# Two batch-0 products and k^T v in quarters of TensorE, lam*beta1 added to the token mix's input, beta2 as a 321st column

## Chip, cores and metric

One core of one Trainium2 chip. The metric is the device time of one execution, in microseconds (us). Engines are named as the profile names them: PE is TensorE (PEld its weight loads), DVE is VectorE, ACT is ScalarE, POOL is GpSimd, SP is SyncE, whose queue issues nearly all DMAs.

## What is computed

Linear attention with a norm per head, followed by a residual MLP-mixer block, for 8 batches, 8 heads, 576 positions, head width 64, model width 512 and hidden width 2048, all in float32 at the borders:

```python
kv = einsum('bhsd,bhse->bhde', k, v)
out = einsum('bhsd,bhde->bhse', q, kv)
x = out / sqrt(mean(out*out, -1) + 1e-6) * g_norm        # to [8, 576, 512]
a1 = alpha1 * x + beta1
u = x + lam * einsum('ts,bsd->btd', w_tok, a1)           # token mix
a2 = alpha2 * u + beta2
y = u + lam * (maximum(a2 @ w_ch1, 0) @ w_ch2)           # channel mix
```

## The kernel before

The kernel is a list of operations that `Prog.op` records with an engine, an estimated cost and the keys read and written; `Prog.plan` simulates the list with those costs several times, gives every operation a priority from how late it may run, shakes the priorities at random by a list of seeds, and fixes the order of each engine's queue and its waits. So every engine runs a fixed order, and a change of any cost or seed may reorder all of it. Where PE has nothing ready before the first channel-mix matmul, the planner puts in matmuls on a tile of zeros (`warm`, L1429).

Each batch goes through these steps. `load_kv` and `load_q` fetch k, v and q: 512 positions in one DMA per tensor (L538, L505), the last 64 positions ("tails") in DMAs of their own (L543, L512; L530 for batch 0). `kv_groups` forms k^T v in fp32: two groups of 16 matmuls with 128 rows and 64 columns (L691; each fp32 matmul shows as two instructions), then one group for the tails in quarters of 64 rows and 64 columns (L701), and ACT and DVE copy the result as a bf16 pair, high and low part (L718, L723, L726). q is split into such a pair (`split_q`, L501 and L582) and transposed, by PE for batch 1 (L605), by SP's transposing DMA from batch 2 on (L591). `qkv_groups` multiplies both (L782 with a second matmul on held weights at L401, tails at L863) and normalizes: square on ACT (L819), sum on DVE (L821), root on ACT, reciprocal on DVE, the normalized x (L840, tails L884), then `rt` or `rtt` = x times alpha1*lam*g in bf16 on DVE (L844, tails L892), and x times g_norm in place on POOL (L848, L895). `rtt` holds the 64 tail rows of even batches in its lower half and those of odd batches in its upper half; one row of the other half holds lam*beta1, and the token weights' matching row holds the row sums of w_tok (`sums`, L1301), so that the fifth 128-row source chunk of the token mix brings in the constant too.

`tok_groups` is the token mix: for two pairs of output chunks five source chunks each, 10 matmuls of 512 columns per pair (L920), and in odd batches one group for the tail rows of both batches, in column halves (L942). DVE adds x (L927), multiplies by alpha2 (L933), and SP's DMA transposes the result to `a2t` (L1037); batches 0 and 1 are transposed on PE instead (`ut_pe`, L1007, evicted at L1016 and L1017). `ch1_groups` is the first layer: 16 groups of 4 matmuls of 512 columns in even batches (L1056), of 8 matmuls of 320 columns in odd ones (L1075), which also take the tails of the batch before; ACT applies the ReLU with the bias `hb` from batch 2 on (L1045, L1046). `hb`, beta2 times w_ch1, is formed in batch 0 with a one-column matmul after each of L1056 on the same weights (`matmul_held`, L401). `ch2_groups` is the second layer (L1121, 64 or 80 matmuls a batch) with the addition (L1131) and the store (L1134). The steps of batch b+1 up to its transposed input are merged among the layers of batch b.

Batch 0 has no layers to hide behind. Its k, v and q come in two halves of four heads. `kv_first` already runs in quarters of TensorE (L628). `qt_first` transposes q by matmuls with the identity, 128 rows by 64 columns (L649; tails L663), and the products q x kv (L789) use a block-diagonal `kv32` that is zeroed at the start. Then come the transposes of w_tok (L1260, L1278; loads L1219 and L1222), the token mix in two column halves (`tok_first`, L972), and the transposes of its result. The weights of both layers are loaded to borrowed buffers and cast (L1340, L501) or multiplied by lam (L1351, L1357).

## Time and profile before

| | us |
|---|---|
| median of 3 runs (368.4 to 368.56) | 368.47 |
| the profiled execution, its own time | 368.05 |
| its span, first to last instruction | 366.2 |
| PE busy, of that span | 360.6 |
| DVE / ACT / POOL busy | 198.4 / 159.2 / 81.7 |
| PE before batch 0's first channel-mix matmul | up to 38.6 |

The views used below: the chain of what ended last (start, length, engine, tile, line and count of each piece), the groups of instructions by line, operation and shape, the timeline, windows (for each stretch its length, then the busy time and count of PE, PEld, DVE, ACT and POOL, the granted TensorE clock, the DMA engines' share and GB/s), and the DMA issues with their time to landing. The granted clock is 1.00 in every stretch of the span.

### The profile page before, as it was taken

To read this page: it belongs to the slowest core of one execution; us is meant where nothing else is said; L and a number is where in the kernel's file an instruction comes from. 1 tells how busy PE (TensorE), PEld (TensorE's weight loads), DVE (VectorE), ACT (ScalarE), POOL (GpSimd) and SP (SyncE) were. 2 spreads that over 40 slices of the span, in tenths; PEclk is the share of its full clock that TensorE was granted. 3 is DMA by queue.
4 is the path that set the end of the run, shared out by engine and by line. 5 is a ranking of instruction groups with operands and counts; after the bars stand their busy time and mean duration, and the time that the engine had idled before them with its cause. 6 is when DMAs were issued, how large, how long until landed. Compare 5 with 4: busy or idle time off the path is not lost.

```text
span 366.2 us, 7069 instructions
## 1 busy us (share of the span) xinstructions
PE 360.6 (98%) x3164; PEld 205.8 (56%) x2876; DVE 198.4 (54%) x313; ACT 159.2 (43%) x268; POOL 81.7 (22%) x71
## 2 busy tenths in 40 slices
PE   7999999999999999999999999999999999999996
PEld 3787445467754554457654554457654554457644
DVE  4287699773973197735764176915933165720021
ACT  2464974237830298107650188107630186007600
POOL 4064602700450007100530006400620006200000
PEclk9999999999999999999999999999999999999999
DMA  8999999999777897439904499233404110420012
GB/s 257 319 290 319 384 382 273 265 250 249 211 141 158 246 259 178 101 94 309 230 18 115 138 304 177 50 110 85 90 7 108 59 30 0 59 100 30 0 57 88
DMA packets 92423, 59.87 MB, mean 163 GB/s; under 512 B 59549, under 2 KB 82341, under 8 KB 92264
## 3 DMA queue, kind: packets, MB, share of 16 engines
q1 hardware_dynamic: 92368, 59.41, 62.5%
q8 instruction: 24, 0.39, 0.5%
q14 instruction: 7, 0.06, 0.0%
q10 hardware_dynamic: 24, 0.01, 0.0%
HBM read 38.56 MB, written 9.44 MB: 131 GB/s over the span
## 4 chain that ended last, share of the span: by engine, by line
PE 97%; DMA 2%; SPq 0%; DVE 0%; issue 0%
PE ps L1121 34%; PE ps L1075 19%; PE ps L1056 16%; PE ps L920 8%; PE ps L691 4%; DMA qf<-in_q_dram 2%; PE ps L401 2%; PE ps L782 2%; PE ps L789 1%; PE ps L942 1%; PE ps L972 1%; PE ps L1007 1%; PE ps L1429 1%; PE ps L649 1%; PE ps L1102 1%; PE ps L701 1%
## 5 line engine op out<-in xcount | busy, mean ns | idle before, releaser
L1121 PE MATMUL ps<-w,ht 128*128 128x512 bf16 x560 | 126.0, 379 | 0.0
L848 POOL TENSOR_TENSOR xm<-xm,g_bc 128x512 f32<-128x512 f32 (+1 forms) x36 | 47.4, 1316 | 186.6 <-DVE rt L844 184.7
L1121 PEld LDWEIGHTS ps<-w,ht 128*128 128x128 bf16 x560 | 53.1, 98 | 63.0 <-issue 1.2
L1045 ACT ACTIVATE ht<-ps,hb 128x512 bf16<-128x512 f32 (+1 forms) x96 | 70.5, 739 | 40.5 <-PE ps L1075 32.8
L1075 PE MATMUL ps<-a2t,w 128*128 128x320 bf16 x512 | 71.9, 299 | 0.0
L1075 PEld LDWEIGHTS ps<-a2t,w 128*128 128x128 bf16 x512 | 49.3, 98 | 20.2 <-ACT ht L1045 0.3
L1056 PE MATMUL ps<-a2t,w 128*128 128x512 bf16 x256 | 59.7, 379 | 0.0
L1131 DVE TENSOR_TENSOR xm<-ps,xm 128x512 f32<-128x512 f32 x31 | 21.4, 689 | 50.4 <-PE ps L1121 50.3
L718 ACT ACTIVATE kvd<-ps 64x128 bf16<-64x128 f32 x28 | 7.6, 271 | 78.5 <-PE ps L701 78.1
L1056 PEld LDWEIGHTS ps<-a2t,w 128*128 128x128 bf16 x256 | 24.3, 97 | 29.6 <-issue 1.2
L821 DVE TENSOR_REDUCE small<-sq 128x16 f32<-128x1024 f32 (+2 forms) x20 | 20.5, 1028 | 22.9 <-ACT sq L819 22.9
L920 PE MATMUL ps<-rt,wt 128*128 128x512 bf16 x112 | 28.8, 379 | 0.0
L501 ACT ACTIVATE qs<-qf 128x1024 bf16<-128x1024 f32 (+1 forms) x15 | 14.2, 964 | 26.7 <-DMA qf<-in_q_dram 26.1
L927 DVE TENSOR_TENSOR xm<-ps,xm 128x1024 f32<-128x1024 f32 x14 | 17.1, 1222 | 14.5 <-PE ps L920 14.5
L1046 ACT ACTIVATE ht<-ps 128x512 bf16<-128x512 f32 (+1 forms) x32 | 20.6, 650 | 6.8 <-PE ps L1075 3.3
L819 ACT ACTIVATE sq<-ps 128x1024 f32<-128x1024 f32 (+2 forms) x20 | 17.4, 873 | 7.3 <-PE ps L789 4.3
L840 DVE TENSOR_TENSOR xm<-ps,small 128x1024 f32<-128x1024 f32 (+1 forms) x18 | 19.8, 1103 | 0.4
L723 DVE TENSOR_TENSOR kvd<-ps,kvd 64x128 bf16<-64x128 f32 x28 | 8.1, 288 | 20.5 <-ACT kvd L718 20.0
L844 DVE TENSOR_TENSOR rt<-xm,e1g_bc 128x1024 bf16<-128x1024 f32 (+1 forms) x17 | 19.0, 1125 | 0.1
L582 DVE TENSOR_TENSOR qs<-qf,qs 128x1024 bf16<-128x1024 f32 x12 | 15.3, 1284 | 6.8 <-ACT qs L501 6.8
L920 PEld LDWEIGHTS ps<-rt,wt 128*128 128x128 bf16 x112 | 10.9, 98 | 12.9 <-issue 0.4
L691 PEld LDWEIGHTS ps<-vf,kf 128*64 128x64 f32 x448 | 14.2, 138 | 5.0 <-issue 5.0
(119 smaller groups left out, 334.2 us busy)
## 6 DMA issues: line engine op xcount, KB each, us to landing
out_dram<-xm SPq DMA_DIRECT2D x31, 256.0 KB, 2.5
kf<-in_k_dram SPq DMA_DIRECT2D x7, 1024.0 KB, 10.3
vf<-in_v_dram SPq DMA_DIRECT2D x7, 1024.0 KB, 8.0
qf<-in_q_dram SPq DMA_DIRECT2D x7, 1024.0 KB, 8.0
stg<-in_moe_w_ch_dram SPq DMA_DIRECT2D x3, 1024.0 KB, 13.8
kf<-in_moe_w_ch_dram SPq DMA_DIRECT2D x2, 1024.0 KB, 14.6
kf<-in_k_dram SPq DMA_DIRECT2D x2, 576.0 KB, 5.2
vf<-in_v_dram SPq DMA_DIRECT2D x2, 576.0 KB, 6.3
```

Source lines behind the costliest of these rows:

```text
L691: m = e.matmul(out(h), kf[:, buf, h, c, :], vf[:, buf, h, c, :], start=(c == 0 and h < 4 * a + 2), stop=False, skip_group_check=True)
L821: P.op("DVE", dve_us(64 * m), lambda e: e.tensor_reduce(out=smv, in_=sqv.rearrange("p (h d) -> p h d", h=m), axis=AX.X, op=ALU.add), r=[(" ...
L840: P.op("DVE", dve_us(64 * m), lambda e: e.tensor_tensor(out=x3, in0=split(raw()), in1=inv, op=ALU.mult), r=[t, ("sm", sms)], w=xk, pri=-200)
L844: lambda e: e.tensor_tensor(out=r_, in0=x, in1=eb, op=ALU.mult),
L848: P.op("POOL", pool_us(64 * nh), lambda e, xc=xc: e.tensor_tensor(out=xc, in0=xc, in1=g_bc[rows, None, :].to_broadcast([nr, nh, DH]), op=A ...
L920: m = e.matmul(t.ap()[:, i, :], tok_w(b, sc, c), rsrc(b, sc), start=(sc == 0), stop=(sc == 4))
L1045: o = P.op("ACT", act_us(n) + 0.09, lambda e: e.activation(dst, src(), ACT.Relu, bias=hb[:, fj:fj + 1]) if b > 1 else e.activation(dst, sr ...
L1046: dst, src(), ACT.Relu, bias=hb[:, fj:fj + 1]) if b > 1 else e.activation(
L1056: m = e.matmul(t.flat(), w, a2t[:, dj, 0:512], start=(dj == 0), stop=(dj == 3))
L1075: m = e.matmul(t.ap()[:, i, 0:320], w1[:, dj, 128 * fj:128 * fj + 128], a2t[:, dj, 320 * i:320 * i + 320], start=(dj == 0), stop=(dj == 3))
L1121: m = e.matmul(t.flat(), ht[:, fj, 128 * c:128 * c + 128], w2[:, fj, :], start=(fj == 0), stop=(fj == 15))
L1131: P.op("DVE", dve_us(512), lambda e: e.tensor_tensor(out=x, in0=t.flat(), in1=x, op=ALU.add), r=[t] + keys, w=keys)
```

## The change

- k and v of batches 1 to 7 come in one DMA each, with the 576 positions as 64 x 9 per head; k^T v (`kv_product`) then runs for all batches as two groups of 36 fp32 matmuls in quarters of 64 rows and 64 columns. The tail tiles and their DMAs and matmuls go.
- For batch 0, the transposes of q run in the same quarters, and the products q x kv in two row halves of 64, without the block-diagonal zeros; `first` issues them in one group of 16 and one of 4 matmuls per half.
- From batch 2 on, DVE multiplies into an fp32 scratch tile, adds lam*beta1 (formed once in `lam_bc`, from one more broadcast load) and writes `rt`/`rtt`; the tail rows are copied to the other half of `rtt` too. POOL's product waits for `rt`. The token mix then has four full source chunks per output chunk, and the last 64 source rows of the two output chunks of a pair as two matmuls on the lower and the upper 64 rows. In the tail group (L942) the last source chunk takes 64 rows.
- The one-column matmuls of batch 0 go; beta2 is column 640 of `a2t`, and the second matmul of each pair in batch 1's first layer has 321 columns. Sixteen one-column copies fill `hb`.
- The keys of x and rt are in quarters instead of halves, some costs and priorities of the planner change, and its seeds are six others instead of one, with another shake.

```diff
-            return {o: pri[o] + (rnd.gauss(0.0, 2.0) if rnd.random() < 0.1 else 0.0)
+            share, by = (0.02, 0.1, 0.3)[seed % 3], (1.0, 3.0)[seed % 2]
+            return {o: pri[o] + (rnd.gauss(0.0, by) if rnd.random() < share else 0.0)
...
-        b2c = sb("b2c", [128, 4], BF16)
...
-        kf = sb("kf", [128, 2, NH, 4, DH], F32)
-        vf = sb("vf", [128, 2, NH, 4, DH], F32)
+        kf = sb("kf", [128, 2, 2304], F32)
+        vf = sb("vf", [128, 2, 2304], F32)
...
-        kft = sb("kft", [128, 2, 4, DH], F32)
-        vft = sb("vft", [128, 2, 4, DH], F32)
...
-        a2t = sb("a2t", [128, 4, TP], BF16)
+        a2t = sb("a2t", [128, 4, TP + 16], BF16)
...
 
-        def load_kv(b, go=()):
+        def load_kv(b):
             j = (b + 1) % 2
-            for tile, tl, src, n in ((kf, kft, k, "kf"), (vf, vft, v, "vf")):
-                P.op("SP", 0.6, lambda e, tile=tile, src=src: e.dma_start(
-                    tile[:, j].rearrange("p h c d -> p h (c d)"),
-                    src[b, :, 0:512, :].rearrange("h (p c) d -> p h (c d)", c=4)),
-                    r=go, w=[(n, j)], dma_us=3.4)
-                for g in range(2):
-                    P.op("SP", 0.5, lambda e, tl=tl, src=src, g=g: e.dma_start(
-                        tl[64 * g:64 * g + 64, j],
-                        src[b, 4 * g:4 * g + 4, 512:576, :].rearrange("h s d -> s h d")),
-                        w=[(n + "t", j, g)], dma_us=0.4)
+            for key, src, tile in (("kf", k, kf), ("vf", v, vf)):
+                P.op("SP", 0.6, lambda e, src=src, tile=tile: e.dma_start(
+                    tile[:, j].rearrange("p (z f) -> p z f", z=4),
+                    src[b].rearrange("(z y) (p c) d -> (y p) z (c d)", y=2, c=9)),
+                    w=[(key, j)], dma_us=3.1)
 
         def load_q(b, hs=ALL[0], tails=True):
             load_main(qf, "qf", q, b, hs)
...
+        def kv_product(b, a):
+            j = a if b == 0 else (b + 1) % 2
+            t = P.ptile(2)
+
+            def f(e):
+                for c in range(9):
+                    for x, y in ((0, 0), (0, 1), (1, 0), (1, 1)):
+                        r = slice(64 * y, 64 * y + 64)
+                        m = e.matmul(t.ap(slice(64 * x, 64 * x + 64))[:, y, 0:64],
+                                     nine(kf, b, a)[r, x, c, :], nine(vf, b, a)[r, x, c, :],
+                                     start=(c == 0), stop=(c == 8), skip_group_check=True)
+                return m
+            P.op("PE", 1.22, f, r=[("kf", j), ("vf", j)], w=[t])
+            return t
...
-                P.op("PE", 1.22, f, r=[("kf", a), ("vf", a)], w=[t])
+                t = kv_product(0, a)
                 for h in range(2):
                     rows = slice(64 * h, 64 * h + 64)
                     P.op("ACT", act_us(128), lambda e, h=h, rows=rows: copy(
-                        e, kv32[rows, 2 * a:2 * a + 2, 64 * h:64 * h + 64],
-                        t.ap(rows)[:, :, 0:64]), r=[t, "kvz"], w=[("kv32", a, h)])
+                        e, kv32[rows, 2 * a:2 * a + 2, 0:64], t.ap(rows)[:, :, 0:64]),
+                        r=[t], w=[("kv32", a, h)])
             for a in range(2):
...
+            def main(a):
+                t = P.ptile(2)
 
                 def f(e):
-                    for c in range(4):
-                        for h in range(2):
-                            m = e.matmul(t.flat(slice(64 * h, 64 * h + 64))[
-                                :, 128 * c:128 * c + 128], qf[:, 4 * (pr // 2) + 2 * h + pr % 2, c, :], ident[:],
-                                start=True, stop=True)
+                    for y in range(2):
+                        for c in range(4):
+                            for x, r in ((0, 0), (0, 1), (1, 0), (1, 1)):
+                                rows = slice(64 * r, 64 * r + 64)
+                                o = 256 * y + 64 * c
+                                m = e.matmul(t.ap(slice(64 * x, 64 * x + 64))[:, r, o:o + 64],
+                                             qf[rows, 4 * a + 2 * x + y, c, :],
+                                             ident[rows, rows], start=True, stop=True)
                     return m
-                P.op("PE", 0.95, f, r=["ident", ("qf", pr // 2)], w=[t])
-                P.op(act_dve(512), 0, lambda e: copy(e, qt32[:, pr, 0:512], t.flat()),
-                     r=[t], w=[("q32", pr)])
+                P.op("PE", 1.12, f, r=["ident", ("qf", a)], w=[t])
...
-            yield tails
+            kv5 = kvd[:].rearrange("p (a x y) i d -> p a x y i d", a=2, x=2)
+
+            def group(a):
+                t = kv_product(b, a)
+                for x in range(2):
+                    own = slice(64 * x, 64 * x + 64)
+                    P.op("ACT", act_us(128), lambda e, x=x, own=own: e.activation(
+                        kv5[own, a, x, :, 0], t.ap(own)[:, :, 0:64], ACT.Identity),
+                        r=[t], w=[("kvd", a, x, 0)])
+                for x in range(2):
+                    own, oth = slice(64 * x, 64 * x + 64), slice(64 - 64 * x, 128 - 64 * x)
+                    P.op("DVE", dve_us(128), lambda e, x=x, own=own: e.tensor_tensor(
+                        out=kv5[own, a, x, :, 1], in0=t.ap(own)[:, :, 0:64],
+                        in1=kv5[own, a, x, :, 0], op=ALU.subtract),
+                        r=[t, ("kvd", a, x, 0)], w=[("kvd", a, x, 1)])
+                    P.op("DVE", 0.22, lambda e, x=x, own=own, oth=oth: e.tensor_copy(
+                        out=kv5[oth, a, x], in_=kv5[own, a, x]),
+                        r=[("kvd", a, x, i) for i in range(2)], w=[("kvd", a, x, 2)], port=True)
+            for a in range(2):
+                yield lambda a=a: group(a)
...
+            def first(hs):
+                a = hs.start // 4
+                aa = [("kv32", a, i) for i in range(2)]
+                ts = [P.ptile(1) for i in range(2)]
+
+                def product(e, o, x, y, lo, n):
+                    r = slice(64 * x, 64 * x + 64)
+                    return e.matmul(o, qt32[r, 2 * a + y, lo:lo + n], kv32[r, 2 * a + y, 0:64],
+                                    start=True, stop=True)
+
+                def f(e):
+                    for c in range(4):
+                        for y in range(2):
+                            for x in range(2):
+                                o = 128 * c + 64 * y
+                                mm = product(e, ts[x].flat()[:, o:o + 64], x, y, 128 * c, 128)
+                    return mm
+                P.op("PE", 1.0, f, r=QT + KVD + aa + [("q32", 2 * a), ("q32", 2 * a + 1)], w=ts)
+                for x, t in enumerate(ts):
+                    h = hs.start + 2 * x
+                    norm(t, (0, 1, 2, 3), slice(h, h + 2))
...
-                    xc = x3[:, i] if nc_ > 1 else x3
-                    P.op("POOL", pool_us(64 * nh), lambda e, xc=xc: e.tensor_tensor(
-                        out=xc, in0=xc, in1=g_bc[rows, None, :].to_broadcast([nr, nh, DH]),
-                        op=ALU.mult), r=xkeys(b, c, hs) + ["g"], w=xkeys(b, c, hs), pri=-50)
+                rk = [kk for c in cs for kk in rkeys(b, c, hs)]
+                if b < 2:
+                    P.op(dve_pool(64 * m) if b == 0 else "DVE", dve_sb(64 * m),
+                         lambda e: e.tensor_tensor(out=r_, in0=x, in1=eb, op=ALU.mult),
+                         r=xk + ["e1"], w=rk, pri=-100, port=True)
+                else:
+                    sv = sqv.rearrange("p (c f) -> p c f", c=nc_)
+                    eb2 = lam_bc[rows, None, lo:hi].to_broadcast([nr, nc_, 64 * nh])
+                    P.op("DVE", dve_sb(64 * m), lambda e: e.tensor_tensor(
+                        out=sv, in0=x, in1=eb, op=ALU.mult), r=xk + ["e1"], w=[("sq", sqs)],
...
+                    P.op("POOL", pool_us(64 * nh * len(cs_)), lambda e, xc=xc, gb=gb: e.tensor_tensor(
+                        out=xc, in0=xc, in1=gb,
+                        op=ALU.mult), r=k2 + ["g"] + (rk if b > 1 else []), w=k2, pri=-50)
             def tail():
...
+                    sv = sq[rows, sqs, 0:512]
+                    P.op("DVE", dve_sb(512), lambda e: e.tensor_tensor(
+                        out=sv, in0=x, in1=e1g_bc[rows, :], op=ALU.mult),
+                        r=xk + ["e1"], w=[("sq", sqs)], pri=-100, port=True)
+                    P.op("DVE", dve_sb(512), lambda e: e.tensor_tensor(
+                        out=rv(b, (4,)), in0=sv, in1=lam_bc[rows, :], op=ALU.add),
+                        r=[("sq", sqs), "e2"], w=rkeys(b, 4), pri=-100, port=True)
+                    oth = slice(64 - lo_, 128 - lo_)
+                    P.op("DVE", 0.3, lambda e: e.tensor_copy(
+                        out=rtt[oth, b % 2, :], in_=rv(b, (4,))),
+                        r=rkeys(b, 4), w=rkeys(b, 4), pri=-100, port=True)
                 P.op("POOL", pool_us(512), lambda e: e.tensor_tensor(
...
+                scs = 5 if b < 2 else 4
                 for i, c in enumerate(cs):
                     def f(e, i=i, c=c):
-                        for sc in range(5):
+                        for sc in range(scs):
                             m = e.matmul(t.ap()[:, i, :], tok_w(b, sc, c), rsrc(b, sc),
                                          start=(sc == 0), stop=(sc == 4))
                         return m
-                    P.op("PE", 1.1, f, r=[kk for s in range(5) for kk in wtk(s, b) + rkeys(b, s)],
-                         w=[t])
+                    P.op("PE", 0.217 * scs, f,
+                         r=[kk for s in range(scs) for kk in wtk(s, b) + rkeys(b, s)], w=[t])
+                if scs < 5:
+                    def g(e):
+                        for i, c in enumerate(cs):
+                            r = slice(64 * i, 64 * i + 64)
+                            m = e.matmul(t.ap()[:, i, :], wt[r, 4 + i, 128 * c:128 * c + 128],
+                                         rtt[r, b % 2, :], start=False, stop=True)
+                        return m
+                    P.op("PE", 0.24, g, r=wtk(4, 0) + wtk(4, 1) + rkeys(b, 4), w=[t])
...
                         for i in range(2):
-                            m = e.matmul(t.flat(slice(64 * i, 64 * i + 64)), tok_w(i, sc, 4),
-                                         rsrc(i, sc), start=(sc == 0), stop=(sc == 4),
+                            w, r = tok_w(i, sc, 4), rsrc(i, sc)
+                            if b > 1 and sc == 4:
+                                w, r = tok_w(0, 4, 4)[0:64], r[0:64]
...
-                    dst, src(), ACT.Relu), r=[t, "hb"] if b > 1 else [t], w=[("ht", fj)])
+                    dst, src(), ACT.Relu), r=[t, ("hb", fj)] if b > 1 else [t], w=[("ht", fj)])
...
-                        if b == 0:
-                            m = P.matmul_held(hbt.flat()[:, fj:fj + 1], w, b2c[:, dj:dj + 1],
-                                              dj == 0, dj == 3)
...
+                            n = 321 if (b, i) == (1, 1) else 320
+                            m = e.matmul(t.ap()[:, i, 0:n],
                                          w1[:, dj, 128 * fj:128 * fj + 128],
-                                         a2t[:, dj, 320 * i:320 * i + 320],
+                                         a2t[:, dj, 320 * i:320 * i + n],
                                          start=(dj == 0), stop=(dj == 3))
                     return m
-                o = P.op("PE", 1.1, f, r=[("w1", fj // 4)] + [("a2t", i) for i in range(5)],
-                         w=[t])
+                o = P.op("PE", 1.1, f, r=[("w1", fj // 4)] + [("a2t", i) for i in range(5)]
+                         + ["b2c"] * (b == 1), w=[t])
                 mark(b, 0, fj, o)
+                if b == 1:
+                    P.op(act_dve(1), 0, lambda e: copy(
+                        e, hb[:, fj:fj + 1], t.ap()[:, 1, 320:321]), r=[t], w=[("hb", fj)])
                 relu(t, lambda: t.ap()[:, :, 0:320],
                      ht[:, fj, :].rearrange("p (a f) -> p a f", a=2), fj, 640)
...
-            P.op("DVE", 0.2, lambda e: e.tensor_copy(out=b2c[:], in_=ta.flat()[:, 4:8]),
+            P.op("DVE", 0.2, lambda e: e.tensor_copy(out=a2t[:, :, TP], in_=ta.flat()[:, 4:8]),
...
-        P.op("DVE", 0.4, lambda e: e.memset(kv32, 0.0), w=["kvz"])
...
+        spread_load(moe_beta1, stg[:, 0, 0, :], "st0")
         P.chain = False
+
+        P.op("DVE", dve_sb(512), lambda e: e.tensor_tensor(
+            out=lam_bc[:], in0=stg[:, 0, 0, :], in1=lam_bc[:], op=ALU.mult),
+            r=["st0"], w=["lam", "e2"], port=True)
 
...
-        P.plan(due, 8, (15,))
+        P.plan(due, 8, (5, 16, 49, 104, 112, 197))
```

216 lines of the change are left out of this document (90 added, 126 removed).

## The prediction

> **What bounds the kernel now.** I read the page first, its span and engine totals:
>
> ```profile
> span 366.2 us, 7069 instructions
> PE 360.6 (98%) x3164; PEld 205.8 (56%) x2876; DVE 198.4 (54%) x313; ACT 159.2 (43%) x268; POOL 81.7 (22%) x71
> ```
>
> Then the view of what each engine waited for (total, times, longest):
>
> ```profile
> PE ps L1429 <- DVE a2b L1226: 1.9, 1, 1.9
> ```
>
> TensorE (PE) is the path: 360.6 of 366.2 us, and its longest wait by far in the view of waits is the 1.9 us at the very start. So an edit is worth what it takes out of PE's own sequence. But "busy" hides two things: filler matmuls (L1429, which multiply zeros while nothing else is ready), and pauses of TensorE between differently shaped matmuls. So next the chain of what ended last, piece by piece (start, length, what, count):
>
> ```profile
> 8.76 1.97 PE ps L649 x32
> ...
> 12.52 1.67 PE ps L789 x12
> 14.19 1.21 PE ps L628 x72
> 15.40 1.09 PE ps L789 x8
> 16.49 1.90 PE ps L649 x32
> 18.65 1.62 PE ps L1429 x7
> 20.27 1.78 PE ps L789 x16
> 22.05 0.48 PE ps L1260 x4
> ...
> 26.60 0.58 PE ps L789 x4
> 27.18 1.64 PE ps L1301 x10
> ...
> 36.69 1.94 PE ps L1429 x9
> ...
> 38.85 0.24 PE ps L1056
> 39.58 0.47 PE ps L605 x8
> ...
> 58.61 12.95 PE ps L1121 x60
> ...
> 93.60 0.37 PE ps L863 x16
> ...
> 120.04 1.08 PE ps L691 x32
> 121.12 1.83 PE ps L1121 x8
> ...
> 125.87 0.39 PE ps L701 x16
> ...
> 145.98 4.32 PE ps L920 x20
> 150.29 1.20 PE ps L942 x10
> ...
> 165.70 3.26 PE ps L1075 x24
> ```
>
> Up to 8.76 PE has little to do but filler. From there to 38.6, where the channel mix of batch 0 begins (L1056), it works on small fp32 products with 3.6 us of filler (1.62 and 1.94) among them. From 38.6 to the end it never pauses for another engine. A 512-column bf16 matmul costs 12.95/60 = 0.216 us there; that is the unit below.
>
> **The change, part by part.**
>
> *beta2 as a 321st column.* Today each of the 64 channel-mix matmuls of batch 0 is followed by a one-column matmul on the same weights:
>
> ```profile
> L401 PE MATMUL ps<-b2c,w 128*128 128x1 bf16 x64 | 10.5, 164 | 0.0
> 57.73 0.18 ACT L501 ACTIVATE hb<-ps 128x16 f32<-128x16 f32 x1
> ```
>
> A pair takes 0.24 us (piece at 38.85), a plain one 0.216: 64 x 0.024 = **1.5 us saved**. One more column of 320 in 64 matmuls of batch 1 costs 64 x 0.135/320 = 0.03 us (3.26/24 = 0.136 each). The one copy of 16 columns becomes 16 copies of one, at 0.18 us as in the row above (the fixed part): 2.9 us on ACT or DVE, spread over batch 1's first layer. I cost them at nothing: both engines are half idle there (windows view, below). Without that cover they cost up to 2.9 us.
>
> *k^T v in quarters.* For batches 1 to 7 two groups of 32 (L691) and one of 16 (L701) become two groups of 72, the form that batch 0 already runs (L628, 1.21 us). What follows such a group also pays: the 8 matmuls of L1121 at 121.12 take 1.83 instead of 8 x 0.216 = 1.73, so each group costs 0.10 us more than its own length. Before: 1.08 + 1.08 + 0.39 + 3 x 0.10 = 2.85. After: 2 x (1.21 + 0.10) = 2.62. Saved 0.23 x 7 = **1.6 us** (bounds 0.7 without a pause saved, 2.3 if the two groups are planned side by side). Copies on ACT and DVE keep their number and shapes.
>
> *Last 64 source rows in two row halves.* For batches 2 to 7, two of each pair's ten 512-column matmuls (L920) become one pair on 64 rows each, side by side. If that were free, it would save 6 x 2 x 0.216 = 2.6 us. But the trace has a 64-row matmul between 128-row ones, in the sums (weight loads of L1301):
>
> ```profile
> 28.07 0.09 PEld L1301 LDWEIGHTS ps<-wt,sel 64*128 64x128 bf16 x1 [0.42 <-issue]
> 28.39 0.31 PEld L1301 LDWEIGHTS ps<-wt,sel 128*128 128x128 bf16 x5 [0.23 <-issue]
> ```
>
> From 28.07 to 28.39 is 0.32 us for one matmul of 0.216. The whole group (27.18) has five 512-column and five 64-column matmuls, 5 x 0.216 + 5 x 0.023 (L863's 0.37/16) = 1.20, and took 1.64: 0.44 for four changes between 128 and 64 rows, 0.11 each. So a half-row pair costs 0.216 + 2 x 0.11 = 0.44 where two full ones cost 0.43: **nothing saved**. The column-half group L942 says the same of its form: 1.20 for five slots of 0.216 = 1.08. In batches 3, 5 and 7 that tails group now ends with 64-row operands, one more change each, 3 x 0.11 = **0.3 us lost**. Bounds: 2.6 gained if row halves enter freely, about 1 gained if the planner puts the two pairs next to each other, 0.5 lost.
>
> [...]
>
> *Transposes and products of batch 0.* 64 instructions in quarters replace two groups of 16 in each L649 piece: 64 x 1.21/72 = 1.08 instead of 1.97 and 1.90, 1.7 us less. The q x kv products go from L789's 1.67 + 1.09 + 1.78 + 0.58 = 5.1 us to 40 instructions per half in row halves, not in the trace: lower bound L628's 1.21/72 each if four ran at once (0.7 per half), upper the 0.11 of L789 per pair (2.2); I take two at once at L691's 1.08/32 = 0.034, so 1.35 + 0.2 per half, 3.1 in all: 2.0 less. This is PE work ahead of the token weights, and those come by DMA:
>
> ```profile
> 7.69 0.49 SPq L1222 DMA_DIRECT2D ht<-in_moe_w_tok_dram  x1
> ...
> ht<-in_moe_w_tok_dram SPq DMA_DIRECT2D x1, 144.0 KB, 11.6
> ```
>
> The second of their two loads is issued at 7.69 and lands 11.6 later, at 19.3; the transposes (L1260) start today at 22.05. What is saved before 19.3 is lost in filler, so the start can gain 22.05 - 19.3 = 2.7 us, and some of the last product piece (26.60, 0.58) goes in front of the landing: **3.0 us saved**. Bounds: 1.0 (the plan keeps the order; only work behind the landing shrinks, 0.58 and some 0.4 of waits) and 5.0 (the filler at 36.69 goes as well).
>
> What is late next is the second quarter of the first-layer weights, and its cast:
>
> ```profile
> 8.85 6.64 SPq L543 DMA_DIRECT2D kft<-in_k_dram  x2
> ...
> 40.22 2.00 ACT L501 ACTIVATE w<-w 128x1024 bf16<-128x1024 f32 x2
> ```
>
> The cast ends at 42.2. Four channel-mix groups after a start at 35.6 (16 x 0.216), with three transpose groups of 0.47 (L605) between them, PE wants it at 40.5: 1.7 us late if it comes as today. But k's tail loads, whose issue holds SP's queue for 6.64 us, and v's like them are ahead of it and go away. I add nothing; the bound is 1.7 lost.
>
> *lam\*beta1, after batch 1.* Each batch from 2 on gets two more 128x1024 operations on DVE, one of 64x512 and a 64-row copy:
>
> ```profile
> L844 DVE TENSOR_TENSOR rt<-xm,e1g_bc 128x1024 bf16<-128x1024 f32 x14 | 16.9, 1206 | 0.1
> 82.90:127.00 44.10, 44.10 (x392) 26.45 (x357) 22.67 (x34) 19.28 (x33) 9.27 (x5) 1.00 0.82 196
> 127.00:165.70 38.70, 38.70 (x322) 19.22 (x288) 26.97 (x40) 18.50 (x33) 8.27 (x6) 1.00 0.67 165
> 143.09 0.97 DVE L892 TENSOR_TENSOR rtt<-xtl,e1g_bc 64x512 bf16<-64x512 f32 x1
> 153.65 3.83 SPq L1037 DMA_TRANSPOSE a2t<-a2b  x3
> a2t<-a2b SPq DMA_TRANSPOSE x5, 2.5
> ```
>
> 2 x 1.21 + 0.97 + about 0.4 for the copy (under half of the 0.97, bf16 both ways) = 3.8 us per batch; DVE goes from 27.0 to 30.8 of 38.7 us in the tighter stage. Behind these on DVE wait POOL's g_norm products, the token-mix addition and the next q splits. Batch 3's tail rows are ready at 144.1, so 147.9 now; PE wants them 8 x 0.216 after it starts the mix at 145.98, at 147.7. It can run second-layer groups first: 64 x 0.216 = 13.8 us of them stand behind. If the mix ends 3.8 later, the transposed input, last issued by 157.5 and there some 2.5 later (160.0), still beats its user at 165.70 by 1.9 us. So **nothing**; without cover, up to 3.8 x 6 = 23 us.
>
> Sum against the profiled execution's 368.05 us (span 366.2 and 1.85 around it): 1.5 + 1.6 - 0.3 + 3.0 = 5.8, giving 362.2. That execution is 0.4 below the median of 368.47, so I say **362.6**.
>
> **The rivals.**
>
> *Row halves enter for free* (2.6 instead of -0.3): 359.7. For it, quarters of L628 start four at once; against it, the 64-row matmul at 28.07. [...]
>
> *The start gains all it can*: both fillers go, 5.0 instead of 3.0: 360.6. For it, kv(1) work can fill the place; against, the eviction of the last transposes still lies between.
>
> *The start hardly gains*: 1.0, so 364.6, or 366.3 if the w1 cast also waits its 1.7. For it: DVE and ACT have the same norms and casts to do in less time. Against: the tail loads go.
>
> *The mix input gets late (slower).* Slack behind the mix is 160.0 to 165.7 = 5.7 us in the stages that end in a five-chunk batch (3, 5, 7). It decides once DVE's order makes of 3.8 us more than 5.7, for instance with four other operations of 1.2 us (q splits, sums) queued in between: 8.6. Then 2.9 x 3 = 8.7 us of PE idleness: 371.3. It eats the whole gain of 5.8 from a delay of 5.7 + 5.8/3 = 7.6 on. For it: DVE has 30.8 of 38.7 us filled there. Against: second-layer groups can go first.
>
> *Nothing comes of it*: the new seeds draw another order of everything, and what the start gains is given back in waits: 368.5.
>
> **How the numbers follow.** Forecast 0.46 (own range 361 to 364); free row halves 0.10; full start 0.16; small start 0.13; late mix 0.08; nothing 0.07. The range leaves out the late mix, "nothing" and a corner of the free halves with a full start: 359.0 to 366.0. A measurement of this kernel tells 0.2% (0.7 us) from no change. Faster: the first four, 0.85; within: over half of the last, 0.04; slower: the late mix and the rest, 0.11.
>
> **What would show it.** L401 without b2c and 16 small hb copies; kv pieces of 1.2 us twice per batch and no 0.39; for the token mix 16 full matmuls in about 3.46 us and two half-row pairs that cost 0.44 each with their changes; the first channel-mix matmul at 35 to 36 us; PE with no waits after it. It is wrong if a filler or a gap stands before a token mix or a first layer, if the half-row pair costs 0.25, or if the first layer starts before 34 or after 37.5.

## The result and the profile after

The changed kernel takes **371.54 us** (median of 4 runs, 371.34 to 371.83) against 368.48 of the kernel before: a ratio of 1.0084 (95% interval 1.0066 to 1.0101), slower by some 3.1 us. Forecast were 362.6 us and a gain. Its profiled execution took 371.5 us, with a span of 369.7.

The page of the kernel after (span, busy time and count of each engine, chain that ended last):

```profile
span 369.7 us, 8109 instructions
...
PE 358.8 (97%) x3660; PEld 203.2 (55%) x3436; DVE 234.0 (63%) x344; ACT 160.7 (43%) x276; POOL 86.1 (23%) x71
...
q8 instruction: 28, 0.46, 0.5%
...
PE 82%; DVE 11%; issue 2%; DMA 2%; SPq 2%; ACT 0%
```

PE has less to do than before (358.8 instead of 360.6 us, fillers counted in), yet the span is 3.5 us longer: PE waits. DVE has 35.6 us more to do and is now 11% of the chain. The view of what PE waited for (total, times, longest) says for whom (a wait of the first microseconds, which the kernel before has too, is left out):

```profile
PE ps L963 <- DVE rtt L921: 2.1, 2, 1.2
PE ps L1477 <- issue: 1.5, 1, 1.5
...
PE ps L954 <- DVE xm L969: 1.2, 1, 1.2
PE ps L622 <- issue: 1.1, 1, 1.1
```

Two kinds of wait are new. The half rows of the token mix (L963) and its full chunks (L954) wait for DVE, and a filler (L1477) and a quarter product (L622) wait for nothing that the profile shows ("issue"). The chain of the start shows the second kind in its place (start, length, what, count):

```profile
17.32 1.09 PE ps L652 x64
18.41 0.54 PE ps L1477 x2
18.95 1.49 issue
20.44 1.67 PE ps L1477 x7
22.11 1.93 PE ps L743 x32
...
36.47 0.97 PE ps L622 x54
37.44 1.10 issue
38.54 0.56 PE ps L622 x18
...
41.00 0.89 PE ps L600 x16
...
42.55 1.73 PE ps L1102 x8
...
44.73 8.63 PE ps L1102 x40
```

The transposes in quarters (L652) took 1.09 us, against 1.08 forecast. But the products of the second half (L743) start at 22.11, about where the w_tok transposes began before, and the first channel-mix matmul comes at 42.4 instead of 38.5.

Where the time went by stages is worked out from the starts of TensorE's matmuls in the traces: first the start of batch 0's first channel-mix matmul, then the distance from each batch's first channel-mix matmul to the next batch's (the last one to the end of PE's work). Later runs stand in the same table. All of it is read from the profiled executions, which can differ from the medians (that of e1, 369.23 us, is the fastest of its ten).

```
                       start |  b0     b1     b2     b3     b4     b5     b6     b7
before                 38.47 | 44.40  44.20  38.47  44.19  38.47  44.19  35.59  34.58
after                  42.39 | 43.01  46.06  38.02  44.10  38.92  43.94  35.38  34.58
e1  no lam*beta1       41.81 | 43.02  44.69  38.22  43.94  38.22  43.94  35.59  34.58
e2  old start          43.87 | 43.79  42.12  38.91  44.23  38.91  43.94  35.39  34.59
e3  old draws          42.00 | 43.28  44.14  38.01  43.94  38.92  43.94  35.39  34.58
e4  before, new draws  41.53 | 43.94  44.20  38.47  44.19  38.47  44.19  35.59  34.58
e5  fillers held       41.45 | 43.01  46.06  38.01  44.06  38.91  43.94  35.39  34.58
e6  no late fillers    41.88 | 43.02  46.06  38.02  43.94  38.91  43.94  35.39  34.58
e7  small g product    42.31 | 43.01  44.76  38.01  44.20  38.01  43.94  35.39  34.58
e8  no add, old first  36.43 | 44.33  44.01  38.22  43.94  38.22  43.94  35.59  34.58
e9  e8 with the add    35.84 | 47.78  43.07  38.91  43.94  38.91  43.94  35.39  34.58
e10 e9, copy on ACT    36.36 | 47.77  44.13  38.01  43.94  38.02  43.94  35.38  34.58
e11 new first          40.89 | 44.89  42.13  38.22  43.94  38.22  43.94  35.59  34.58
e12 e10, other order   39.01 | 41.51  44.00  38.30  43.95  38.01  43.94  35.39  34.58
```

After against before: the start loses 3.92 us. Of these 1.34 are 24 transposes of L600 that the new order puts ahead of the channel mix (16 in 0.89 us at 41.00 in the chain, 8 more in 0.45 behind them); stage b0 gets them back. It should have gained 1.5 from the one-column matmuls and 0.25 from k^T v as well, and falls by 1.39 only: a wait of 1.61 us at 75.64, which comes up again with e7, stands in it. So the start is 2.6 us worse, b1 is 1.86 worse, b4 0.45; b2, b3, b5 and b6 are 0.1 to 0.45 better. Together +3.8, of which the end behind PE's last matmul gives 0.3 back.

### The profile page after: what moved, and what is told of

It reads as the page before. It is cut to its first block, busy times and chain, and to the rows that moved or that the text cites. A ratio compares the mean times of both kernels' runs of the same rounds, so it can differ in the third digit from the quotient of the medians.

```text
span 369.7 us, 8109 instructions
## 1 busy us (share of the span) xinstructions
PE 358.8 (97%) x3660; PEld 203.2 (55%) x3436; DVE 234.0 (63%) x344; ACT 160.7 (43%) x276; POOL 86.1 (23%) x71
## 4 chain that ended last, share of the span: by engine, by line
PE 82%; DVE 11%; issue 2%; DMA 2%; SPq 2%; ACT 0%
PE ps L1162 30%; PE ps L1102 14%; PE ps L1117 12%; PE ps L622 5%; PE ps L954 4%; PE ps L1477 3%; DVE qs L577 3%; DMA out_dram<-xm 2%; PE ps L780 2%; PE ps L402 2%; SPq L512 1%; PE ps L743 1%; PE ps L1017 1%; PE ps L1052 1%; PE ps L987 1%
## 5 line engine op out<-in xcount | busy, mean ns | idle before, releaser
L864 POOL TENSOR_TENSOR xm<-xm,g_bc 128x512 f32<-128x512 f32 (+1 forms) x36 | 53.5, 1487 | 207.9 <-DVE rt L853 177.2
L1117 PE MATMUL ps<-a2t,w 128*128 128x320 bf16 (+1 forms) x512 | 72.5, 299 | 0.5 <-DVE xm L838 0.5
L1102 PE MATMUL ps<-a2t,w 128*128 128x512 bf16 x256 | 58.1, 379 | 0.0
L954 PE MATMUL ps<-rt,wt 128*128 128x512 bf16 x112 | 26.3, 379 | 1.2 <-DVE xm L969 1.2
L622 PEld LDWEIGHTS ps<-vf,kf 64*64 64x64 f32 x1152 | 18.4, 135 | 6.8 <-issue 6.0
L577 DVE TENSOR_TENSOR qs<-qf,qs 128x1024 bf16<-128x1024 f32 (+1 forms) x14 | 22.0, 1578 | 0.1
L622 PE MATMUL ps<-vf,kf 64*64 64x64 f32 x1152 | 20.8, 221 | 1.1 <-issue 1.1
L969 DVE TENSOR_TENSOR xm<-ps,xm 128x1024 f32<-128x1024 f32 x14 | 16.8, 1218 | 4.6 <-PE ps L963 4.5
L954 PEld LDWEIGHTS ps<-rt,wt 128*128 128x128 bf16 x112 | 10.6, 98 | 14.2 <-DVE xm L969 1.7
```

The lines of the kernel that those rows point to most:

```text
L577: lambda e, hi=hi, lo=lo, src=src: e.tensor_tensor(out=lo, in0=src, in1=hi, op=ALU.subtract), r=kin + kh, w=kl, port=True)
L622: m = e.matmul(t.ap(slice(64 * x, 64 * x + 64))[:, y, 0:64], nine(kf, b, a)[r, x, c, :], nine(vf, b, a)[r, x, c, :], start=(c == 0), stop= ...
L864: P.op("POOL", pool_us(64 * nh * len(cs_)), lambda e, xc=xc, gb=gb: e.tensor_tensor(out=xc, in0=xc, in1=gb, op=ALU.mult), r=k2 + ["g"] + ( ...
L954: m = e.matmul(t.ap()[:, i, :], tok_w(b, sc, c), rsrc(b, sc), start=(sc == 0), stop=(sc == 4))
L1102: m = e.matmul(t.flat(), w, a2t[:, dj, 0:512], start=(dj == 0), stop=(dj == 3))
L1117: m = e.matmul(t.ap()[:, i, 0:n], w1[:, dj, 128 * fj:128 * fj + 128], a2t[:, dj, 320 * i:320 * i + n], start=(dj == 0), stop=(dj == 3))
```

## The experiments

All times are medians; the ratio is to the kernel before, run on the same chip, with its 95% interval.

| run | us | ratio |
|---|---|---|
| e1 no lam\*beta1 | 370.22 | 1.0059 (1.0035 to 1.0084) |
| e2 old start | 370.78 | 1.0054 (1.0036 to 1.0072) |
| e3 old draws | 369.69 | 1.0039 (1.0012 to 1.0067) |
| e4 before with the new draws | 370.88 | 1.0069 (1.0054 to 1.0084) |
| e5 fillers held | 371.09 | 1.0072 (1.0051 to 1.0092) |
| e6 no late fillers | 370.63 | 1.0063 (1.0048 to 1.0078) |
| e7 small g product | 369.29 | 1.0020 (1.0005 to 1.0035) |
| e8 no add, old first products | 364.38 | 0.9890 (0.9876 to 0.9905) |
| e9 e8 and the add | 367.84 | 0.9979 (0.9970 to 0.9988) |
| e10 e9, copy on ScalarE | 367.00 | 0.9960 (0.9945 to 0.9975) |
| e11 new first products, no add | 367.91 | 1.0000 (0.9975 to 1.0024) |
| e12 e10, another order | 363.88 | 0.9881 (0.9864 to 0.9897) |

### Which part: e1 to e4

e1: the kernel after with the token mix of before.

```diff
-                if b < 2:
+                if True:
...
-                scs = 5 if b < 2 else 4
+                scs = 5
...
-        spread_load(moe_beta1, stg[:, 0, 0, :], "st0")
```

> The changed kernel with the token mix of before: no lam*beta1 addition, no copy of the tail rows, five full source chunks, the constant through the row sums again. All else and the seeds as changed. Late-mix theory (DVE's added operations run beside POOL's g_norm products and come late): PE's gaps before the token mixes of batches 2 and 5 (1.4 and 1.0 us) go, DVE falls from 234 to about 205 us busy, and the time falls from 371.5 to 368-369.5. Start theory: the two gaps at 18.6 and 37.2 us stay, so at least 2.9 us of the loss stay. Order theory (the new seeds order everything badly, the parts matter little): 370.5-372.

e2: the kernel after with batch 0's query transposes and first products as before.

```diff
-            def main(a):
+            def pair(pr):
...
-            def first(hs):
+            def group32(cs, hs):
```

> The changed kernel with batch 0's q transposes and q x kv products as before (128 rows by 64 columns, block-diagonal kv). Start theory (PE runs out of instructions, because quarters need 128 and 144 instructions in 1.1 to 1.2 us and the next block of 256 comes late behind data): with fewer instructions the gaps of 1.65 and 1.27 us in the first 42 us go or fall under 0.5; the fp32 work grows by 2.1 us; the first channel-mix matmul at 41-43 and the time 370-371.5. Late-mix theory: nothing changes after the start, 371.5 plus the 2.1 of work less filler. Order theory: a shift of either sign by 1-2 us with gaps in new places.

e3: the kernel after, its order drawn as before was; e4: the kernel before, its order drawn as after was.

```diff
-            share, by = (0.02, 0.1, 0.3)[seed % 3], (1.0, 3.0)[seed % 2]
-            return {o: pri[o] + (rnd.gauss(0.0, by) if rnd.random() < share else 0.0)
+            return {o: pri[o] + (rnd.gauss(0.0, 2.0) if rnd.random() < 0.1 else 0.0)
...
-        P.plan(due, 8, (5, 16, 49, 104, 112, 197))
+        P.plan(due, 8, (15,))
```

> The changed kernel with the seed and the shake of before, all operations as changed. Order theory: the loss was in the new seeds; time at 363-365.5, as the sum of the parts says. Late-mix theory: PE gaps before token mixes of 3 us or more in all remain, 368-371. Start theory: a PE gap of 1 us or more behind instruction 705 (and at steps of 256 from there) remains wherever DMA is full and quarters ran ahead of it.

> The kernel before with the shake and the six seeds of the changed kernel, no operation changed. Order theory: 370-372, as the changed kernel. Late-mix and start theories: 368.5 within 1.5, no PE gap over 0.5 us after the first channel-mix matmul.

None of the four reaches 368.4. Without the add (e1) stage b1 is 1.4 us shorter and b4 0.7, but half-row savings of 0.2 in b2 and b6 go too, and the start is nearly as late as ever; 370.22 lies between the ranges of two theories and decides for neither alone. The old start operations under the new seeds (e2) don't mend the start either: 43.87, later than expected. e4 is the sharpest: before's own operations in another order lose 3.06 us at the start and get 0.46 back in b0, 370.88 us. So the order alone, which I had listed as "nothing comes of it", can cost 2.5 us. But it isn't the whole: e3, in the draws of before, starts at 42.00 and takes 369.69 us, not the 363 to 365.5 of the order theory.

### The wait that nothing explains: e5 and e6

The two "issue" waits of after stand where PE has started 705 and 1217 instructions (matmuls, weight loads and semaphore instructions counted in the trace). 705 = 193 + 2 x 256 and 1217 = 193 + 4 x 256. The queue of kind "instruction" in the page above moved 0.46 MB in 28 packets, 16 KB each, for PE's 7146 instructions: 255 a packet (before it was 24 packets for 6109). I read it as 256 instructions a packet, since the two waits lie 512 instructions apart. The packets around the first wait, from the trace:

```
        packet on its way   instructions started when it     wait behind instruction 705
                            was sent / when it had landed
after   18.11 to 19.20           688 / 705                   18.57 to 20.44
before  20.08 to 21.26           532 / 554                   none (705 comes at 29.70)
e8      19.05 to 20.11           665 / 676                   none
```

As I read it, PE used up the instructions that it had, and the next block came 18 to 19 us into the start, behind data that keep the DMA engines busy throughout (a share of 1.04 from 18 to 21 us): PE went on 1.24 us after the packet had landed. Before, the same 705 instructions lasted until 29.7; quarters of 64 matmuls and 64 weight loads per 1.09 us use them up sooner.

The traces also say how long a block lasted where PE had to wait and where it hadn't. In all fourteen kernels a packet is sent 2.0 to 4.6 us after PE has started the first instruction behind 193, and again behind 449 (behind 705 and 961 it is 2.2 to 7.4). Where PE had to wait for the next block, it went on 4.5 to 7.1 us after the start of the block before, in most cases 5.4 to 6.2. The block from 449 to 705 lasted 13.3 us before, 6.0 in e8 and 3.8 in after, where PE went on after 5.7. That each packet carries the block after the next boundary is a reading of these times, not something that the profile names.

e5 changes only the number of instructions: fillers that follow a filler keep their weights, without a weight load.

```diff
+        prev = None
+        for o in P.order["PE"]:
+            mine = o.tiles and o.tiles[0] is P.warm[3]
+            if mine and prev:
+                o.fn = lambda e: P.matmul_held(P.warm[3].flat(), wz[:, 0:128], wz, True, True)
+            prev = mine
```

> The kernel after with its own order, but a filler that directly follows a filler keeps the weights that are loaded already and issues no weight load: about 20 TensorE instructions fewer by the first wait that no semaphore explains (1.87 us between two instructions at 18.57), about 31 fewer by the second (1.32 us at 37.22). Theory of instruction blocks (TensorE has used up its block of 256 instructions and the next one, asked for at 15.23, lands at 19.20 behind the data): the first wait falls below 0.3 us, since the block then ends in the fillers or the products behind 20.5; the second falls only a little, to 0.9 to 1.3, since it ends inside the same quarter products; first channel-mix matmul at 40.3 to 40.9 instead of 42.39; 369.6 to 370.2 us. Rival (the data set the start, the block wait hides inside a wait for data): a gap of the same size returns before an instruction with a semaphore, the first channel-mix matmul stays at 42.2 to 42.6, 371.2 to 371.9 us.

e6 takes the 27 late fillers out of after's order.

```diff
+        late = [o for o in P.order["PE"] if o.tiles and o.tiles[0] is P.warm[3] and o.start > 8.5]
+        for f in late:
+            for o in P.ops:
+                if f in o.deps:
+                    o.deps.remove(f)
+                    o.deps |= f.deps
+        P.order["PE"] = [o for o in P.order["PE"] if o not in late]
+        P.sequence = [o for o in P.sequence if o not in late]
```

> The kernel after with its own order, less the 27 fillers that stand behind 8.5 us (they took 8.00 us of TensorE, a wait of 1.87 us among it); nothing else is moved. Theory that the fixed fillers set the start: the work behind them moves up until data stop it, the first channel-mix matmul comes at 38 to 40 instead of 42.39, and 367.2 to 369.2 us. Rival (the fillers stand where the data aren't there yet): gaps with semaphores take their place, the first channel-mix matmul comes at 41.5 to 42.5, and 370.7 to 371.8 us; a granted clock below that of after in the first 40 us would say that the fillers kept the clock up.

In e5 the wait left the filler at 18.57 and came back smaller, 0.63 us between two of the first products at 21.00, the chain of e5:

```profile
20.69 0.59 PE ps L743 x6
21.28 0.36 issue
21.63 1.67 PE ps L743 x25
```

It is again the place behind instruction 705: other work, later time, same count. The second wait, 1.14 us between two instructions, is again behind 1217. The first channel-mix matmul moved up by 0.94 us, the time by 0.45 with an interval that overlaps that of after, so the size isn't settled: less than the 1.3 to 1.9 expected. In e1, e3, e6, e7 and e11 a wait stands behind 705 too, in e2 behind 961, in e12 behind 1217. e6 has a short one behind 449 too (0.73 us); e1, e6 and e7 have one behind 1217 as well, and so do e9 and e10 (1.2 us, 5.5 us after the block before; there the profile names a copy on DVE for 1.0 of it).

e6 lies at the edge of its rival (41.88 and 370.63 us), far from the first theory, and the reason is in the last clause of its expectation. Without fillers PE stands idle between quarter transposes and products, 1.3 us for two copies on ScalarE and then the block's wait; its windows, below those of after (length, then busy time and count of PE, PEld, DVE, ACT, POOL, then granted clock, DMA share, GB/s):

```profile
18.00:21.00 3.00, 1.51 (x33) 0.77 (x26) 2.97 (x7) 1.23 (x3) 1.73 (x3) 1.00 1.04 405
24.00:27.00 3.00, 3.00 (x29) 2.59 (x28) 2.12 (x5) 2.20 (x6) 0.17 (x1) 1.00 1.09 373
```

```profile
18.00:21.00 3.00, 1.00 (x13) 0.85 (x13) 1.85 (x3) 0.00 (x1) 2.76 (x4) 0.65 1.03 400
21.00:24.00 3.00, 2.97 (x22) 2.86 (x23) 0.00 (x0) 0.54 (x2) 1.72 (x3) 0.50 1.05 409
24.00:27.00 3.00, 3.00 (x22) 2.38 (x21) 2.10 (x4) 1.18 (x5) 0.00 (x0) 0.50 1.08 380
27.00:30.00 3.00, 3.00 (x18) 2.32 (x17) 2.18 (x6) 2.35 (x6) 0.57 (x1) 0.64 1.10 327
```

The granted clock falls to 0.50 for 6 us, so that 16 of the w_tok transposes take 3.53 us instead of some 2.1 (8 in 1.16 and 8 in 0.92 in after). The 27 fillers, 8 us with the first wait among them, had kept the full clock (1.00 in all of after's windows); taking them away gained 0.5 us at the start. What they'd be worth without that loss can't be read from this run.

### The late additions: e7

GpSimd's product with g covers 64 of 512 columns from batch 2 on; order and waits stay.

```diff
+                    xc = xc[:, 0:1] if b > 1 else xc
...
+                    gb = gb[:, 0:1] if b > 1 else gb
```

> The kernel after with its own order and waits, but GpSimd's product with g is done on the first 64 of 512 columns alone from batch 2 on (what is left out: the product on the other 448 columns). Theory that VectorE's added operations are slow because GpSimd's products run beside them: the add of the tail rows falls from 1.34 to about 0.7 us mean, the copy of the tail rows from 1.13 to about 0.55, the adds on full rows from 1.2 to near 1.0 or below; the gaps of 1.62 us before the half rows at 108.32 and 1.21 us at 235.56 vanish; the gap of 1.61 us at 75.64 (batch 1, whose product with g is whole) stays; 368.0 to 369.3 us. Rival (the operations are slow by their own form, two bfloat16 operands or a partition shift): their durations stay within 0.1 us, the gaps stay, 371.2 to 371.9 us.

In the kernel after, the timeline of DVE and then of POOL around the wait at 108.3 (start, length, engine, line, operation, tiles, shapes):

```profile
104.59 1.21 DVE L577 TENSOR_TENSOR qs<-qf,qs 128x1024 bf16<-128x1024 f32 x1
105.72 0.68 DVE L917 TENSOR_TENSOR rtt<-sq,lam_bc 64x512 bf16<-64x512 f32 x1
106.33 2.28 DVE L577 TENSOR_TENSOR qs<-qf,qs 128x1024 bf16<-128x1024 f32 x1
108.64 1.25 DVE L921 COPY rtt<-rtt 64x512 bf16<-64x512 bf16 x1
```

```profile
104.15 5.59 POOL L864 TENSOR_TENSOR xm<-xm,g_bc 128x512 f32<-128x512 f32 x2 [1.38 <-DVE rt L853]
109.81 1.26 POOL L924 TENSOR_TENSOR xtl<-xtl,g_bc 64x512 f32<-64x512 f32 x1
```

POOL's two products take 5.59 us (3.38 and 2.12), where two of the same shape at 64.0 take 2.62, and of the two q splits beside them one takes 1.21, as at 126.19 with POOL idle (1.22), the other 2.28: here the engines hold each other up. The half rows wait for the copy, which ends at 109.9. The same groups by shape, after and then e7 (busy, mean ns of one):

```profile
L577 DVE TENSOR_TENSOR qs<-qf,qs 128x1024 bf16<-128x1024 f32 x12 | 20.7, 1728 | 0.1
L969 DVE TENSOR_TENSOR xm<-ps,xm 128x1024 f32<-128x1024 f32 x14 | 16.8, 1218 | 4.6 <-PE ps L963 4.5
L850 DVE TENSOR_TENSOR sq<-xm,e1g_bc 128x1024 f32<-128x1024 f32 x12 | 14.5, 1208 | 0.0
L917 DVE TENSOR_TENSOR rtt<-sq,lam_bc 64x512 bf16<-64x512 f32 x6 | 8.1, 1344 | 0.1
L921 DVE COPY rtt<-rtt 64x512 bf16<-64x512 bf16 x6 | 6.8, 1129 | 0.2
```

```profile
L577 DVE TENSOR_TENSOR qs<-qf,qs 128x1024 bf16<-128x1024 f32 x12 | 16.8, 1407 | 0.1
L919 DVE TENSOR_TENSOR rtt<-sq,lam_bc 64x512 bf16<-64x512 f32 x6 | 4.3, 711 | 0.1
L923 DVE COPY rtt<-rtt 64x512 bf16<-64x512 bf16 x6 | 1.8, 298 | 0.2
```

As expected by the first theory: the copy falls from 1129 to 298 ns, the tail add from 1344 to 711, and both gaps before the half rows are gone; stage b1 is 1.30 us shorter, b4 0.91, the time 2.25, to 369.29. The rival, slow by their form, is out. One number was wrong: the operations on full rows (L850, L853) are 1.21 in both; these weren't slowed; POOL's product of the same rows waits for them. Nor is the mix's addition, with one input from PSUM: L969 takes 1.22 us in both kernels, and 1.21 in the two of after's 14 that lie beside POOL (238.35 and 321.43).

The gap at 75.64 (1.61 us, L954 waiting for L969) stayed, as expected, since batch 1's product was left whole: two q splits of 4.43 us stand in front of the mix's addition there. e1 has it too (75.06, 1.61), so it comes from the order and from the splits beside POOL's products (4.40 us for two in e1), not from the additions of lam\*beta1.

### Parts put together again: e8 to e12

e8 keeps the 321st column, k^T v in quarters and the query transposes in quarters; first products, token mix and the draws are those of before, with the seed 12.

```diff
-            def first(hs):
+            def group32(cs, hs):
...
-                if b < 2:
+                if True:
...
-        P.plan(due, 8, (5, 16, 49, 104, 112, 197))
+        P.plan(due, 8, (12,))
```

> Not the whole change: the 321st column, k^T v in quarters, and the query transposes in quarters of batch 0, with the old token mix (no lam*beta1 added, nothing copied) and the old first products, and an order drawn with another seed (12, by the draws of before). By the terms: from 368.05 profiled, held matmuls -1.5, quarters of k^T v 7 x -0.25 = -1.75, start between 0 (the order meets the same data) and -1: 364.8 and a little over it, 364.0 to 365.5 us, first channel-mix matmul at 37.5 to 38.5. If every order but that of before loses its start to fillers and to a wait for instructions (first channel-mix matmul at 40.5 to 42): 366.5 to 368.5 us.

364.38 us: the terms that I had worked out for these parts, 364.8, hold, and with them the view of PE as the path. The start gains 2.04 us against before (36.43), 1.1 more than I had expected of e8 at best and two thirds of the 3.0 forecast for the change; a wait of 1.61 us at 79.15, for the eviction of transposes on DVE, takes most of that surplus back. In the chain of its start, fillers stand between transposes and products, and no wait:

```profile
16.24 0.93 PE ps L651 x64
...
17.76 1.62 PE ps L1465 x7
19.38 0.58 PE ps L745 x4
...
20.28 1.78 PE ps L745 x16
22.06 0.48 PE ps L1295 x4
...
28.70 0.65 PE ps L1465 x3
...
36.27 0.32 PE ps L1465
```

This chain also says that the gain isn't the one forecast. The token weights land at 19.04 in e8 and their transposes (L1295) begin at 22.06, where they began at 22.05 before: all that the quarter transposes of q saved went into fillers. The 2.04 us lie behind that point: the last product piece (0.58) stands in front of it now, 0.97 less filler is needed (1.94 before), and the other pieces are some 0.5 shorter.

e9 adds the token mix of the change to e8; e10 is e9 with the copy on ScalarE; e12 is e10 with seed 0.

```diff
-                    P.op("DVE", 0.3, lambda e: e.tensor_copy(
-                        out=rtt[oth, b % 2, :], in_=rv(b, (4,))),
-                        r=rkeys(b, 4), w=rkeys(b, 4), pri=-100, port=True)
+                    P.op("ACT", act_us(512), lambda e: copy(
+                        e, rtt[oth, b % 2, :], rv(b, (4,))),
+                        r=rkeys(b, 4), w=rkeys(b, 4), pri=-100)
```

> e8 and the token mix of the change on top of it (lam*beta1 added from batch 2 on, the tail rows copied, row halves), with the order's seed of e8, so that the start is that of e8 (first channel-mix matmul at 36.2 to 36.7): this edit alone. As predicted blind (the added operations lie beside other work): half rows save 0.2 us in batches 2, 4 and 6 (38.22 to 38.02 in the runs so far), 363.4 to 364.2 us. Theory that they are slowed beside GpSimd's product and come late: the copy is again 1.0 to 1.25 us and the tail add 1.3 to 1.7, one or two gaps of 0.8 to 1.7 us stand before the half rows or a first layer, 365.0 to 367.0 us.

> e9 with the copy of the tail rows on ScalarE instead of VectorE. Theory of VectorE beside GpSimd: the copy no longer takes 1.1 to 1.25 us (on ScalarE 0.6 to 0.7), the half rows' wait is shorter by 0.4 to 0.8 us at each gap, 0.4 to 1.6 us below e9, 363.4 to 365.5 us. If the lateness comes from the chain of operations whatever their engine: within 0.4 us of e9.

> e10 with another order (seed 0), to tell what an order is worth with the same operations: if the start is again without a wait for instructions and first channel-mix matmul stands at 36.5 to 38.5, 362.5 to 364.8 us; with the start of after (41 to 42.5) 366 to 368.5 us.

With the add and the order drawn anew, e9 takes 3.46 us more than e8 (367.84), which is above the range of both theories' forecasts (the late one had 365.0 to 367.0). The waits of e9 and then of e10:

```profile
PE ps L954 <- DVE rtt L911: 1.7, 2, 0.8
PE ps L945 <- DVE xm L960: 1.6, 1, 1.6
PE ps L1043 <- DVE xm L960: 1.3, 1, 1.3
```

```profile
PE ps L945 <- DVE xm L960: 1.6, 1, 1.6
PE ps L1043 <- DVE xm L960: 1.3, 1, 1.3
PE ps L945 <- ACT ht L1083: 0.9, 1, 0.9
```

The wait for the copy (1.7) is gone in e10, and b2 and b4 are 0.90 and 0.89 shorter: in these stages the copy beside POOL was the whole loss. In b1 1.06 come back, most of it a wait for a relu on ScalarE (0.9), and the start is 0.52 later; so 0.2 is left between the two profiled executions (367.45 and 367.27), 0.84 between the medians. The other two waits, 1.97 and 1.59 us at 74.7 and 79.2, stand before the token mix of batch 1, where nothing is added yet: the product lam\*beta1 itself (0.69), the q splits (3.43 for two) and the mix's addition come one after another on DVE. With the wait behind 1217, which falls into b0 here, they are most of b0's 3.45 us over e8, and the additions of batches 2 to 7 have no part in them. With another order of the same operations (e12) both are gone, and **363.88 us** is the best of all, though it can't be told from e8 (0.9881 against 0.9890). Its start, 39.01, lies between the two that were expected, and has the wait behind 1217 (1.59 us).

e11 has the new first products but no add, with the old draws and seed 20.

```diff
-                if b < 2:
+                if True:
...
-        P.plan(due, 8, (5, 16, 49, 104, 112, 197))
+        P.plan(due, 8, (20,))
```

> Without the lam*beta1 add, but with the new first products of batch 0 (two row halves of 64 columns, 80 instructions more before the channel mix than in e8) and the best order that the old draws found for it (seed 20). Theory of instruction blocks: a wait of 1.5 to 2.5 us behind the 705th TensorE instruction at 18 to 19, first channel-mix matmul at 39.5 to 41.5, 366.5 to 368.5 us. Theory that only the order of after and e1 was unlucky: no such wait, first channel-mix matmul at 36.5 to 38.5, 363.8 to 365.8 us.

367.91 us, 3.5 above e8, with the first channel-mix matmul at 40.89. The chain of its start:

```profile
16.82 1.09 PE ps L651 x64
17.91 0.54 PE ps L1472 x2
18.45 1.89 issue
20.35 1.46 PE ps L1472 x6
21.80 2.31 PE ps L742 x40
```

The wait is back behind instruction 705. It stands among the fillers, and yet nothing hides it: the order is fixed, so the six fillers that were to cover the copies run after the wait, not during it. Of the 4.46 us against e8's start, 2.05 are the later end of the first products (24.11 against 22.06), 0.89 are 16 transposes moved ahead, and some 1.2 are more fillers behind 24.11 (2.0 against 0.9). Whether the new first products always bring more fillers, or this order does, stays open.

## Why the prediction was wrong

Two terms were right in size, and a third in its mechanism. **The 321st column**: 40 channel-mix matmuls of batch 0 take 8.63 us (the last row of the chain of after), 0.216 each instead of 0.24; times 64 it is the 1.5 us. **k^T v in quarters**: stage b5 falls from 44.19 to 43.94 in every run with it, 0.25 against the 0.23 forecast. **Half rows**: b2 and b6 fall by 0.2 against the old token mix (38.22 to 38.02, 35.59 to 35.39), b3 and b5 by nothing; forecast was 0.3 lost in all, so it is about 0.6 gained, far from the 2.6 of the rival. From the starts of the matmuls in after: a pair between full ones takes 0.32 us and about 0.1 from its neighbours, near the 0.44 forecast, and saves nothing in batches 2, 4 and 6. In batches 3, 5 and 7 the planner put both pairs side by side, 0.54 us for the two, which the prediction had as a bound and not in the sum; the tail group there grew from 1.20 to 1.32, as forecast.

**The start, -3.0, was +2.6.** The step that failed is "the start can gain 22.05 - 19.3 = 2.7": it let the token weights' landing alone bound the products' end. Three other things bounded it. First the products themselves, mis-sized: I took 0.034 us for two at once, 3.1 us in all; in the trace of after they and their tails take 4.63 us between them, 1.93 for 32, 0.12 per pair, which was the upper bound I had put. Second the two waits for a block of instructions, 1.9 and 1.3 us from one instruction to the next. I had counted the quarters' time and not their number; the page has 8109 instructions instead of 7069. Third the fillers that the fixed order holds: summed over the trace from 8.6 us to the channel mix, and without the first wait, they take 6.35 us instead of 3.78. The transposes' own saving was as forecast (two times 1.09 against 1.97 and 1.90 us), and yet e8, where the first two causes are absent, didn't bring the token weights' transposes forward at all (22.06 against 22.05, weights landed at 19.04): the second half's products, held back by fillers, stand in front of them in the fixed order. That e8 still starts 2.0 of the 3.0 earlier is luck: it comes from the filler and the product piece behind that point, which were in the bounds and not in the 2.7. That the other orders tried on the full change begin late as well (e3, 42.0) is shown; that e4 does so without a new operation is shown too; so order and blocks each cost, and how the 5.6 us between forecast and result at after's start divide between them isn't settled to better than a microsecond.

**lam\*beta1, "nothing", cost some 2 us in after.** The step that failed is the cover: the added operations were taken to lie beside other work. The two waits for the copy are 1.62 and 1.21 us; with what the half rows save taken off, after lies 1.3 above e1 by the medians and 2.3 by the profiled executions, and e7 gets 2.25 back. e9 lies 3.46 above e8, but of its waits only the 1.7 us for the copy stand where something is added. Nor is the cost bound to the operations: with the copy on ScalarE and another order, e12's stages b1 to b6 are 0.3 us shorter in all than those of e8. Its duration was too low, 3.8 us per batch against 2 x 1.21 + 0.69 + 1.34 + 1.13 less the 0.9 of the old operation, 4.7; but that is the smaller part. I looked for the point of lateness at the transposed input, with 5.7 us of slack, and let second-layer groups go first. It decided two steps earlier: at the half rows, which wait for the copy of the tail rows, and at the mix's first addition, which stands behind the q splits. PE's order doesn't change when they come late. The rival "the mix input gets late" named the place and the sign; its price (8.7 us, from a delay of 5.7 on) came from the wrong slack, and that its 371.3 lies so near the result is luck, since the start made 2.6 us of the loss. And the trace of before had a warning that I didn't read: the tail multiply that I quoted from it took 0.97 beside a product of POOL (142.25 to 145.19), and an operation of its shape takes 0.71 in e7, with POOL's products cut short.

The sum of the terms as measured: start +2.6, held matmuls -1.5, k^T v -1.5 in the stages, half rows -0.6, PE's waits for DVE 1.61 + 0.81 + 1.62 + 1.21 = +5.25 (the first two, at 75.64 and 97.28, have their like in e1, 1.61 and 0.84, and so aren't the additions'): +4.3 where the stages give +3.8; where the 0.5 between them lies is not shown.

## What to carry to other kernels

Before an operation is costed at nothing because its engine is half idle, look at what runs beside it: a copy that takes 0.30 us with GpSimd's products cut short (e7) took 1.25 beside them in full, and the consumer in a fixed order waited for all of it. When small matmuls replace larger ones, count instructions, not only time: at a start that keeps the DMA engines busy (a share of 1.04), quarters in groups of 64 matmuls and 64 weight loads per 1.09 us, with twice as many product instructions around them, used up 256 instructions in 3.8 us where the next 256 took 5.7 to come; in e8, with the old products, they lasted 6.0 and nothing waited. And when an edit brings a new order with it, put each part in a good order before judging it: the same operations gave 367.0 and 363.9 us here (e10 and e12).

## What the runs showed of the hardware

- In the kernel after, 28 packets of 16 KB of the instruction queue stand beside 7146 TensorE instructions, 255 a packet. With the DMA engines at a share of 1.04 (405 GB/s), a packet sent at 18.11 landed at 19.20 and PE went on at 20.44; the waits stand behind instruction 705, 961 or 1217 (in e6 also 449), with a filler there in after and a first product in e5. The block from 449 to 705 lasted 3.8 us in after, with a wait, and 6.0 in e8 and 13.3 before, without one.
- A filler is not idle time with another name: with the 27 late ones the granted clock was 1.00 from 21 to 27 us (after), without them 0.50 (e6).
- VectorE and GpSimd slowed each other in the kernel after: two products of GpSimd took 5.59 us instead of 2.62, and one of VectorE's two splits beside them 2.28 instead of 1.21; the copy of the tail rows took 1129 ns in the mean, and 298 in e7 with GpSimd's products cut short.
